# The 64x64 inverses of a chunked delta rule: substitution on 16x16 diagonal blocks instead of a Newton iteration

## The chip, the cores and the metric

The kernel runs on one core of a Trainium2 chip. The metric is the device time of one execution in microseconds (us); the fast executions of one kernel mostly agree within about 1%. Each experiment was timed in rounds beside the kernel before, on the same chip. The kernel before had a median of 325.67 us (323.14 to 328.43, three runs) when the change was predicted, and between 324.0 and 326.3 us in every later comparison.

## The reference

Causal linear attention with the delta rule (4 batches, 8 heads, 768 steps, head size 48), followed by an MLP over 3072 tokens (384 to 2048 to 384, GELU with tanh):

```python
k_n = k / (np.linalg.norm(k, axis=-1, keepdims=True) + 1e-06)
for t in range(S):
    y[:, :, t] = einsum('bhd,bhde->bhe', q[:, :, t], state)
    v_old = einsum('bhde,bhd->bhe', state, k_n[:, :, t])
    state = state + beta[:, :, t] * outer(k_n[:, :, t], v[:, :, t] - v_old)   # cut: index notation
x = y.transpose(0, 2, 1, 3).reshape(B * S, H * D)
out = gelu_tanh(x @ w_in) @ w_out
```

## The kernel before

The kernel works on chunks of 64 steps, 12 of them, with all 32 heads of a chunk at once: 16 head pairs, the two heads of a pair on partitions 0 to 63 and 64 to 127. Within a chunk the recursion is a triangular system: with the Gram matrix G of the 64 keys, the kernel needs the inverse T of (I + strict lower part of beta times G), one 64x64 matrix per head. T times R (values minus what the old state predicts) gives U, from which the new state S and the output x follow. One MLP tile takes the x of two chunks.

Before, T comes from a Newton iteration, five rounds of two products for each half of the heads:

```python
for j in range(5):                                   # cut: names of buffers, priorities
    op(..., {"pe": prod(h1, Zo, X)})                 # 16 products of 64x64
    op(..., {"dve": f_tt(F, 2I, v1(h1), ALU.subtract)})
    op(..., {"pe": prod(h2, F, Zo)})                 # 16 products of 64x64
    op(..., {"act": f_act(Z_next or TT, v1(h2))})
```

No instruction order is written by hand. Every operation is declared with an estimated cost for each engine that may run it, what it reads and writes, and a priority; a list scheduler in Python simulates the engines with these costs and fixes the order in which each engine's instructions stand:

```python
op(cost, fns, reads=..., writes=..., prio=..., alloc=[(bank, n)], dma=...)
...
P.schedule()      # one static order per engine, from the estimated costs
P.emit()          # semaphores between the engines
```

So each engine's list is fixed before the run. What that does shows in the timeline of the changed kernel further below: a product that TensorE had finished at about 251.1 us was read by VectorE only at 254.19, behind a transpose of 4.52 us.

Of the kernel before, what the change touches and what calls it, by code (L numbers as in the profile page):

```python
# [15 lines left out]
KEEP = 0.0  # L16
# [3 lines left out]

class Op:
    __slots__ = ("idx", "cost", "fns", "deps", "prio", "alloc", "uses", "dma", "lat",
                 "eng", "start", "end", "count", "clock", "sync", "mode", "bw")


class Plan:
# [14 lines left out]
    def op(self, cost, fns, reads=(), writes=(), prio=0.0, alloc=(), dma=None, lat=0.0, mode="t", bw=0.0):  # L41
        o = Op()
        o.idx = len(self.ops)
        o.cost, o.fns, o.prio, o.dma, o.lat, o.mode, o.bw = cost, fns, prio, dma, lat, mode, bw
        o.alloc = tuple(alloc)
        o.sync = set()
# [8 lines left out]
        for b in writes:  # L55
            if b in self.last_w:
                deps.add(self.last_w[b])
            deps.update(self.readers.get(b, ()))
# [14 lines left out]
    def schedule(self):  # L73
# [16 lines left out]
        pe_mode = "t"  # L90
# [28 lines left out]
        while n_left:  # L119
            pick = None  # L120
            for e in ENGINES:
# [3 lines left out]
                for i in ready[e]:  # L125
# [4 lines left out]
                    bb = []  # L130
                    if o.alloc:
                        ok = True
                        taken = []
                        for h, n in o.alloc:
                            sv = [(k, bank_free[k]) for k in taken]
                            for k in taken:
                                bank_free[k] = None
                            f = find_banks(n, t, *BANKS[o.mode])
                            for k, x in sv:
                                bank_free[k] = x  # L140
                            if f is None:
                                ok = False
                                break
                            bb.append((h, f[1], n))
                            taken += list(range(f[1], f[1] + n))
                            t = max(t, f[2] + 0.15)
                        if not ok:
                            continue
                    late = max(0.0, t - free_at[e])
                    pr = o.prio  # L150
                    if e == "pe" and (o.mode == "t") != (pe_mode == "t"):
                        pr += KEEP
                    far = late > NEAR[e]
                    key = (far, t if far else 0.0, pr, i)
                    if best is None or key < best[0]:
                        best = (key, i, t, bb)
# [6 lines left out]
            _, i, t, bb, e = pick  # L163
            o = ops[i]
            if e == "pe" and (o.mode == "t") != (pe_mode == "t"):
                t += SWITCH
                pe_mode = o.mode
            o.eng, o.start, o.end = e, t, t + o.cost[e]
# [31 lines left out]
    def emit(self):  # L200
# [21 lines left out]
        for _ in range(len(ops)):  # L222
# [12 lines left out]
            for d in o.deps | o.sync:  # L235
                p = ops[d]
                if p.eng == "pe" and e == "pe" and not p.dma:
# [74 lines left out]
def d_ps(n):  # L312
    return {"dve": 0.13 + 1.07e-3 * n}


def d_any(n):
    return {"act": 0.18 + 0.83e-3 * n, "dve": 0.13 + 1.07e-3 * n}
# [6 lines left out]
def d_pool2(n):  # L324
    return {"pool": 0.10 + 2.0e-3 * n}


def bass_deltanet__then__act_gelu_tanh_kernel(
# [12 lines left out]
    NP = NH // 2  # L341
    NCH = S // C
# [10 lines left out]
    with nc.allow_non_contiguous_dma("head rows"), nc.allow_low_precision("bf16 matmuls"):  # L353
# [3 lines left out]

        identF = sb("identF", [128, 128], F32)
        mU128 = sb("mU128", [128, 128], F32)
        idI = sb("idI", [128, 64], F32)  # L360
        mU = sb("mU", [128, 64], F32)
        half = sb("half", [128, NP], F32)
        BL = sb("BL", [128, 3, 2, 64], F32)
        bcol = sb("bcol", [128, NP, NCH], F32)
        RL, RB, NSQ = 3, 3, 3
        identB = sb("identB", [128, 64], BF16)
        twoI = sb("twoI", [128, 64], BF16)
# [3 lines left out]
        sq = [sb(f"sq{i}", [128, NP, D], F32) for i in range(2)]  # L371
# [3 lines left out]
        KQ = [sb(f"KQ{i}", [128, 2, NP, 64], BF16) for i in range(RB)]  # L375
        KQT = [sb(f"KQT{i}", [128, 2, NP // 2, 128], BF16) for i in range(RB)]
        NU = [sb(f"NU{i}", [128, NP, C], F32) for i in range(2)]

        def ring(nm, n, w):
            return [[[sb(f"{nm}{i}{g}{j}", [128, 8, w], BF16) for j in range(n)] for g in range(2)] for i in range(RB)]  # L380

        Nb, Wb, Xb, Zb, Fb = ring("N", 1, C), ring("W", 1, C), ring("X", 1, C), ring("Z", 2, C), ring("F", 1, C)
        DTb = [sb(f"DT{i}", [128, NP, C], BF16) for i in range(RB)]
        TT = [sb(f"TT{i}", [128, NP, C], BF16) for i in range(RB)]
        Rb = [sb(f"R{i}", [128, NP, D], BF16) for i in range(2)]
        Ub = [sb(f"U{i}", [128, NP, D], BF16) for i in range(2)]
        Sb = [sb(f"S{i}", [128, NP, D], BF16) for i in range(2)]
        x = sb("x", [128, 2, B, DM], BF16)
        xT = sb("xT", [128, 2, B * KT, 128], BF16)
# [19 lines left out]

        def aff(dst, cmp_, fill, pat, cm):  # L410
            return lambda g: g.affine_select(out=dst, in_=dst, compare_op=cmp_, fill=fill, base=0,
# [5 lines left out]

        op({"dve": 0.1}, {"dve": lambda e: e.memset(half[:, :], 0.5)}, writes=["half"], prio=-100)
        for i in range(RB):
            op({"dve": 0.7}, {"dve": lambda e, i=i: e.memset(KQ[i][:, :, :, D:64], 0.0)},  # L420
               writes=[f"KQz{i}"], prio=-90 + i)
        const("identF", identF, 0.0, ALU.not_equal, 1.0, [[-1, 128]], 1)
        const("mU128", mU128, 1.0, ALU.is_gt, 0.0, [[1, 128]], -1)
        for nm, big, sm in (("idI", identF, idI), ("mU", mU128, mU)):
            bn = {"mU": "mU128", "idI": "identF"}[nm]
            for a in range(2):
                r = slice(64 * a, 64 * a + 64)
                op({"dve": 0.1}, {"dve": f_cp(sm[r, :], big[r, r])}, reads=[bn], writes=[nm + str(a)], prio=-80)
        MASKU, IDI = ["mU0", "mU1"], ["idI0", "idI1"]
        op({"dve": 0.1}, {"dve": f_cp(identB[:, :], idI[:, :])}, reads=IDI, writes=["identB"], prio=-80)  # L430
        op({"dve": 0.1}, {"dve": lambda e: e.tensor_scalar(twoI[:, :], idI[:, :], 2.0, None, op0=ALU.mult)},
           reads=IDI, writes=["twoI"], prio=-80)

        bulk = []
# [14 lines left out]
        w1v = moe_w_in.rearrange("(kt p) f -> p kt f", p=128)  # L449
        w2v = moe_w_out.rearrange("(fc p) e -> p fc e", p=128)  # L450

        def load_w(nm, j, pr):
            if nm == "W1":
                dst, src, bw = W1[:, j, :], w1v[:, j, :], 2.9
            else:
                dst, src, bw = W2[:, 4 * j:4 * j + 4, :], w2v[:, 4 * j:4 * j + 4, :], 2.2
            op({"pool": 0.8}, {"pool": f_dma(dst, src)}, reads=gate(), writes=[f"{nm}{j}"], prio=pr,
               dma=f"d_{nm}{j}", bw=bw)
            bulk.append([f"{nm}{j}"])
# [13 lines left out]
        W1N = [f"W1{kt}" for kt in range(KT)]  # L473
        W2N = [f"W2{j}" for j in range(4)]

# [7 lines left out]
        op({"pe": 1.0}, {"pe": f_mms(bt_mms)}, mode="f", reads=["BL0", "BL1", "identF"], writes=[hb_ + (0,), hb_ + (1,)], alloc=[(hb_, 1)], prio=-50)  # L483
        for a in range(2):
            r = slice(64 * a, 64 * a + 64)
            op({"dve": 0.35}, {"dve": f_cp(bcol[r, :, :], lambda a=a, r=r: bank(hb_)[r, 0:NH * NCH].rearrange(
                "q (p a c) -> q p a c", a=2, c=NCH)[:, :, a, :])}, reads=[hb_ + (a,)], writes=[f"bcol{a}"], prio=-49)
        BCOL = ["bcol0", "bcol1"]


        def prep(c):
            s, i, j = c % RL, c % RB, c % 2
            pr = T(c, -STEP)
            kn = [f"kf{s}_0", f"kf{s}_1"]
            parts = [slice(0, 8), slice(8, 16)] if c == 0 else [slice(0, NP)]
            for n, u in enumerate(parts):
# [3 lines left out]
                op(cost, {"pool": f_tt(sq[j][:, u, :], kf[s][:, u, :], kf[s][:, u, :], ALU.mult),  # L500
                          "act": f_act(sq[j][:, u, :], kf[s][:, u, :], ACT.Square)},
                   reads=kn, writes=[f"sq{j}{n}"], prio=pr)
                op({"dve": 0.95 * w}, {"dve": lambda e, u=u: e.tensor_reduce(ss[j][:, u], sq[j][:, u, :], AX.X, ALU.add)},  # L503
                   reads=[f"sq{j}{n}"], writes=[f"ss{j}{n}"], prio=pr)
            ssn = [f"ss{j}{n}" for n in range(len(parts))]
            if c < NSQ:
# [9 lines left out]
            for n, u in enumerate(parts):  # L516
                w = 1.0 / len(parts)
                f = f_tt(KQ[i][:, 0, u, 0:D], kf[s][:, u, :],
                         rn[j][:, u].unsqueeze(2).to_broadcast([128, NP // len(parts), D]), ALU.mult)
                op({"dve": 0.9 * w} if c == 0 and n == 0 else {"pool": 1.5 * w}, {"pool": f, "dve": f},  # L520
                   reads=kn + [f"rn{j}", f"KQz{i}"], writes=[f"KQ{i}" if n == 0 else f"KQx{i}"], prio=pr)
            op({"pool": 0.85, "act": 0.82}, {"pool": f_cp(KQ[i][:, 1, :, 0:D], qf[s][:, :, :]),
                                             "act": f_act(KQ[i][:, 1, :, 0:D], qf[s][:, :, :])},
               reads=[f"qf{s}_0", f"qf{s}_1", f"KQz{i}"], writes=[f"KQq{i}"], prio=pr + 0.1)
            op({"sp": 1.1}, {"sp": f_dma(KQT[i].rearrange("p k m t -> p (k m) t"),
                                         KQ[i].rearrange("p k n d -> p (k n d)"), True)},
               reads=[f"KQ{i}", f"KQq{i}"] + ([f"KQx{i}"] if c == 0 else []), writes=[f"KQT{i}"], prio=pr + 0.2 if c > 1 else -50 + c, dma=f"d_T{c}", bw=1.5)

        def masks(c):
            j = c % 2  # L530
            pr = T(c, -STEP)
            op(d_pool2(NP * C), {"pool": f_tt(NU[j][:, :, :], mU[:, :].unsqueeze(1).to_broadcast([128, NP, C]),
                                              bcol[:, :, c:c + 1].to_broadcast([128, NP, C]), ALU.mult)},
               reads=MASKU + BCOL, writes=[f"NU{j}"], prio=pr + 0.3)

        def mm_pe(n_ins, cols, tiles=2):
            t = max(31.0, cols / 2.4 + 3.0) / tiles
            return {"pe": 1e-3 * n_ins * max(8.3, t)}
# [276 lines left out]
```

## Time and profile before

| kernel before | |
|---|---|
| time, median | 325.67 us |
| profiled span | 322.0 us |
| TensorE busy, products | 272.2 us, 7158 |
| VectorE, ScalarE, GpSimd busy | 175.0, 175.3, 127.1 us |
| start of R,TT of chunks 0, 1, 2, 3, 11 | 38.5, 60.4, 81.1, 112.6, 284.5 us |

The group R,TT (the product of T and R) occurs once per chunk, so its start is a milestone. The text speaks of a head (up to chunk 3), a steady stage (chunks 3 to 11) and a tail (MLP alone). In lines of the profile PE is TensorE (PEld its weight loads), DVE VectorE, ACT ScalarE, POOL GpSimd and SP SyncE, which issues transfers; a q marks an engine's instruction queue, and L with a number is a line of the kernel. One more line of the page before: the chain of work that ended last, by engine, as shares of the span.

```profile
PE 51%; DMA 22%; issue 7%; DVE 7%; ACT 5%; SPq 4%; POOL 2%; POOLq 0%
```

Half of the chain is TensorE, and VectorE has 7% of it.

### The profile page before, as it was taken

Reading aid. Unit: us, or ns where it says so; the run is one execution under the profiler, and the core shown is the slowest. Engines: PE = TensorE matmul, PEld = TensorE weight load, DVE = VectorE, ACT = ScalarE, POOL = GpSimd, SP = SyncE. Lnnn points to the kernel's source line nnn. Section 1 sums busy time; section 2 is a strip of 40 time slices with the busy share of each in tenths; the row PEclk is TensorE's granted clock in tenths of the full one; section 3 lists DMA queues with packets and bytes.
Section 4 is the critical chain, followed back from the end, with each engine's and each line's share of the span. In section 5 each row is a group of like instructions: output and inputs, shape, how many; then the busy total and the mean of one; then the engine's idle time right before and its main releaser. Section 6 shows DMA issues by size and latency. Waiting matters only on the chain.

```text
span 322.0 us, 15234 instructions
## 1 busy us (share of the span) xinstructions
PE 272.2 (85%) x7158; PEld 178.4 (55%) x7158; DVE 175.0 (54%) x279; ACT 175.3 (54%) x309; POOL 127.1 (39%) x96
## 2 busy tenths in 40 slices
PE   1158745988859789999899979989999999989995
PEld 1147644656636466666556556555566556544662
DVE  3489723767557467766775566674556554320111
ACT  4325543668447578634778443777345774168330
POOL 2842330877987257455546371260202211000000
PEclk9998775779998799999999999999999999999999
DMA  7998889879998435495557541709001002101022
GB/s 134 168 182 169 131 119 180 155 151 172 170 176 139 93 69 102 85 181 111 111 100 107 113 103 51 118 4 118 26 29 53 2 9 48 66 36 24 24 75 49
DMA packets 116206, 31.84 MB, mean 99 GB/s; under 512 B 110640, under 2 KB 115760, under 8 KB 116144
## 3 DMA queue, kind: packets, MB, share of 16 engines
q1 hardware_dynamic: 113600, 27.73, 45.5%
q0 software_dynamic: 2544, 3.15, 6.8%
q8 instruction: 56, 0.92, 1.2%
q14 instruction: 6, 0.05, 0.0%
HBM read 20.64 MB, written 4.72 MB: 79 GB/s over the span
## 4 chain that ended last, share of the span: by engine, by line
PE 51%; DMA 22%; issue 7%; DVE 7%; ACT 5%; SPq 4%; POOL 2%; POOLq 0%
PE ps L301 50%; DMA kf<-in_k_dram 8%; DMA qf<-in_q_dram 6%; DMA vf<-in_v_dram 4%; SPq L309 4%; DMA xT<-x 2%; DVE F L285 2%; DMA KQT<-KQ 1%; ACT Z L294 1%; ACT sq L294 1%; ACT x L294 1%; PE ps L600 1%; POOL sr L285 1%; DVE ss L503 1%; DVE R L285 1%
## 5 line engine op out<-in xcount | busy, mean ns | idle before, releaser
L285 DVE TENSOR_TENSOR F<-twoI,ps 128x512 bf16<-128x512 bf16 x120 | 80.4, 684 | 58.4 <-PE ps L301 57.7
L301 PE MATMUL ps<-xT,W 128*128 128x512 bf16 (+1 forms) x336 | 80.6, 364 | 1.8 <-ACT gT L294 1.0
L294 ACT ACTIVATE Z<-ps 128x512 bf16<-128x512 f32 x96 | 56.2, 595 | 42.3 <-PE ps L301 41.5
L294 ACT ACTIVATE gT<-ps 128x512 bf16<-128x512 f32 (+1 forms) x112 | 58.2, 536 | 32.3 <-PE ps L301 31.2
L301 PE MATMUL ps<-W,gT 128*128 128x384 bf16 x384 | 70.0, 327 | 0.6 <-ACT gT L294 0.6
L301 PE MATMUL ps<-X,Z 64*64 64x64 bf16 x1920 | 53.9, 201 | 12.8 <-ACT Z L294 6.9
L301 PE MATMUL ps<-Z,F 64*64 64x64 bf16 x1920 | 54.7, 201 | 8.7 <-DVE F L285 4.0
L301 PEld LDWEIGHTS ps<-X,Z 64*64 64x64 bf16 x1920 | 42.8, 116 | 29.8 <-ACT Z L294 15.1
L301 PEld LDWEIGHTS ps<-Z,F 64*64 64x64 bf16 x1920 | 43.0, 115 | 28.7 <-DVE F L285 15.8
L285 POOL TENSOR_TENSOR W<-identB,N 128x512 bf16<-128x512 bf16 x20 | 23.0, 1151 | 81.8 <-DVE N L285 78.1
L301 PEld LDWEIGHTS ps<-W,gT 128*128 128x128 bf16 x384 | 34.5, 98 | 21.8 <-ACT gT L294 0.8
L301 PEld LDWEIGHTS ps<-xT,W 128*128 128x128 bf16 x336 | 26.7, 100 | 23.1 <-ACT gT L294 4.2
L290 DVE COPY osb<-ps 128x384 f32<-128x384 f32 x20 | 11.1, 557 | 41.3 <-PE ps L301 41.3
L285 POOL TENSOR_TENSOR sr<-ss,half 128x16 f32<-128x16 f32 x9 | 26.2, 2911 | 5.4 <-DVE ss L503 5.2
L285 POOL TENSOR_TENSOR KQ<-kf,rn 128x768 bf16<-128x768 f32 (+1 forms) x12 | 17.1, 1423 | 21.2 <-PE ps L301 16.9
L285 POOL TENSOR_TENSOR NU<-mU,bcol 128x1024 f32<-128x1024 f32 x12 | 23.6, 1971 | 4.4 <-DVE N L285 4.0
L294 ACT ACTIVATE x<-ps 64x768 bf16<-64x768 f32 x24 | 19.3, 804 | 8.2 <-PE ps L301 7.9
L285 POOL TENSOR_TENSOR Z<-identB,N 128x512 bf16<-128x512 bf16 x20 | 23.0, 1151 | 0.0
L294 ACT ACTIVATE TT<-ps 128x512 bf16<-128x512 f32 x24 | 14.3, 596 | 13.4 <-PE ps L301 13.4
L294 ACT ACTIVATE X<-ps 128x512 bf16<-128x512 bf16 x24 | 14.3, 595 | 12.9 <-PE ps L600 12.9
L285 DVE TENSOR_TENSOR N<-ps,NU 128x512 bf16<-128x512 f32 x24 | 16.3, 686 | 8.6 <-PE ps L301 8.6
L301 PE MATMUL ps<-KQT 48*64 48x128 bf16 x384 | 12.7, 246 | 6.6 <-DMA KQT<-KQ 6.4
(49 smaller groups left out, 202.4 us busy)
## 6 DMA issues: line engine op xcount, KB each, us to landing
kf<-in_k_dram SPq DMA_DIRECT2D x24, 192.0 KB, 4.0
qf<-in_q_dram SPq DMA_DIRECT2D x24, 192.0 KB, 3.9
vf<-in_v_dram SPq DMA_DIRECT2D x24, 192.0 KB, 4.3
out_dram<-osb SPq DMA_DIRECT2D x20, 192.0 KB, 1.9
W<-in_moe_w_in_dram POOLq DMA_DIRECT2D x3, 512.0 KB, 6.0
W<-in_moe_w_out_dram POOLq DMA_DIRECT2D x4, 384.0 KB, 7.1
out_dram<-osb SPq DMA_DIRECT2D x8, 96.0 KB, 2.7
BL<-in_beta_dram SPq DMA_DIRECT2D x2, 96.0 KB, 3.6
```

The costliest lines, as they stand in the source:

```text
L285: return lambda e: e.tensor_tensor(out() if callable(out) else out, a() if callable(a) else a, b() if callable(b) else b, op)
L290: return lambda e: e.tensor_copy(out, a() if callable(a) else a)
L294: return lambda e: e.activation(out, a() if callable(a) else a, func)
L301: ins = t.matmul(out, lhsT, rhs, start=st, stop=sp_, skip_group_check=skip)
L309: return lambda e: e.dma_start(out, a)
L503: op({"dve": 0.95 * w}, {"dve": lambda e, u=u: e.tensor_reduce(ss[j][:, u], sq[j][:, u, :], AX.X, ALU.add)}, reads=[f"sq{j}{n}"], writes=[ ...
L600: ins = t.transpose(bankb()[r, p, :], W[r, p, :], identB[r, :])
```

## The change

The intent is to take work off TensorE. T is built from 16x16 diagonal blocks, which are inverted by substitution on GpSimd (VectorE for chunk 0), for two chunks at a time, a "pair". The kernel lays each block in one partition for that. So the 32x32 Gram blocks go through 32x32-block transposes on VectorE (Tt), then come 14 dependent steps of one multiplication and one addition, then two copies (XW, on ScalarE and GpSimd) and two transposes back (Dc). Two expansions (DI, WB) and four short block products on TensorE make T of it.

```diff
+            op({"dve": 1.25}, {"dve": lambda e: e.transpose(
+                Tt[j].rearrange("q (y x) i j -> q x j y i", y=2),
+                Gd[j].rearrange("q c p (x j) -> q x j c p", x=2))}, reads=nG, writes=[f"Tt{j}"], prio=pr)
+            sb_op(512, f_tt(X[:, :, :, :], Tt[j][:, 0:4:3, :, :], bM[j][:, :, :, :], ALU.mult), ...)
+            for s in range(14, 0, -1):
+                w = 15 - s
+                sb_op(2 * s * w, f_tt(tv, X[..., s:s+1], X[:, :, s:s+1, s+1:16], ALU.mult), ...)   # cut
+                sb_op(2 * s * w, f_tt(X[:, :, 0:s, s+1:16], X[:, :, 0:s, s+1:16], tv, ALU.add), ...)
+            ...
+            op({"act": 0.65}, {"act": f_act(XW[j][0].rearrange("q c b r -> q b r c"), X[:, :, :, :])}, ...)
+            for w in (1, 0):
+                op({"dve": 0.7}, {"dve": lambda e, w=w: e.transpose(
+                    Dc[j][w].rearrange("q c p j -> q j (c p)"), XW[j][w].rearrange("q j b i -> q j (b i)"))}, ...)
-            for j in range(5):
-                op(mm_pe(16, 64), {"pe": prod(h1, Zo, X)}, ...)        # cut: the Newton iteration
```

The rest, cut here: the scheduler gets a model of TensorE's instruction fetch (it counts 3.7 us for a block of 256 instructions; the 3.7 is the model's own number, and 2 x 7158 TensorE instructions over the 56 packets on the page before are 256 a packet), x is written transposed and completed by six small transfers per tile instead of one transposing transfer, the first three chunks transpose K and Q on TensorE, U,DT goes on four tiles of the array, W1 comes in eight loads instead of three, and the scheduler prefers to keep TensorE on a run of MLP products for at least 1.2 us and has a few other cost constants. All of this is in the kernel after; no run takes one of these parts away except the fetch model.

## The prediction

> **What bounds the kernel now.** I read the page's engine shares first, then its slices, the costliest groups, the waits of TensorE, and last the timeline of TensorE in the steady part.
>
> The engine shares and three rows of the slices (40 slices of 8.05 us each, busy tenths; the clock row is the granted TensorE clock):
>
> ```profile
> PE 272.2 (85%) x7158; PEld 178.4 (55%) x7158; DVE 175.0 (54%) x279; ACT 175.3 (54%) x309; POOL 127.1 (39%) x96
> ...
> PE   1158745988859789999899979989999999989995
> ...
> PEclk9998775779998799999999999999999999999999
> DMA  7998889879998435495557541709001002101022
> ```
>
> There are two stages. Up to slice 13 (about 105 us) the transfers are at 7 to 9 tenths and TensorE has holes, at a reduced clock. From slice 14 on TensorE is at 9 tenths, the clock is full and every other engine is below 8. So the head waits for data and chains of short operations, and the other 200 us are TensorE's instruction stream. The costliest groups say what that stream is (busy us, mean ns of one; the means contain pipeline overlap):
>
> ```profile
> L301 PE MATMUL ps<-X,Z 64*64 64x64 bf16 x1920 | 53.9, 201 | 12.8 <-ACT Z L294 6.9
> L301 PE MATMUL ps<-Z,F 64*64 64x64 bf16 x1920 | 54.7, 201 | 8.7 <-DVE F L285 4.0
> ```
>
> The two products of the Newton iteration for the 64x64 inverses are 3840 of 7158 matmuls and 109 of 272 busy us. Because ends of matmuls are modelled, I take costs from start to start in the timeline of TensorE (start us, duration us):
>
> ```profile
> 211.48 0.44 PE L301 MATMUL ps<-Z,F 64*64 64x64 bf16 x16
> 211.75 0.42 PE L301 MATMUL ps<-X,Z 64*64 64x64 bf16 x16
> 212.01 0.42 PE L600 MATMUL ps<-identB,W 64*64 64x64 bf16 x16
> ...
> 235.24 0.69 PE L301 MATMUL ps<-R,TT 64*64 64x48 bf16 x32
> 235.77 0.42 PE L301 MATMUL ps<-X,Z 64*64 64x64 bf16 x16
> 236.12 1.48 PE L301 MATMUL ps<-W,gT 128*128 128x384 bf16 x8
> 237.52 0.44 PE L301 MATMUL ps<-U,KQ 64*64 64x48 bf16 x32
> 237.80 0.66 PE L301 MATMUL ps<-U,DT 64*64 64x48 bf16 x32
> 238.30 0.42 PE L301 MATMUL ps<-Z,F 64*64 64x64 bf16 x16
> ```
>
> So 16 small products cost 0.27 us; 32 of them on two tiles of the array (R,TT) 0.53, on four tiles (U,KQ) 0.28. A run of 8 MLP products of N=384 occupies 1.40. Runs of N=512 occupy 0.75 for 3 and 1.40 for 6, so one is 0.216 and each run pays 0.10 once more than its products: the change between large and small products. The change back costs the same: X,Z at 235.77 is followed after 0.35, not 0.27. That leaves 0.163 for one of N=384; N=256 scales to 0.109.
>
> Check: a chunk is 64 time steps of all 32 heads, and an MLP tile takes the outputs of two chunks. A chunk before is 20 x 0.27 (Newton) + 2 x 0.27 (transposes) + 2 x 0.27 (Gram) + 0.53 + 0.51 + 3 x 0.28 = 8.3; its MLP share is (48 x 0.216 + 64 x 0.163) / 2 = 10.4; 224 changes over 12 chunks give 1.9. Sum 20.6. Measured: the R,TT groups start at 112.6 (chunk 3) and 284.5 (chunk 11), 21.5 per chunk. The steady stage is explained by TensorE's own instructions to 5%.
>
> [...] The queue of instructions (packets, MB, share of the 16 engines), and one row of the waits of TensorE (us in total, times, longest):
>
> ```profile
> q8 instruction: 56, 0.92, 1.2%
> PE ps L301 <- issue: 12.7, 12, 4.0
> ```
>
> [...] The second line is a wait of TensorE: 12.7 us in 12 stops, the longest 4.0, that no engine explains; I take them for blocks not yet there.
> [...] The trace has 827 ns against 558 for the 128x384 product KQ<-kf,rn, 1.5x. [...] a 128x16 tensor-scalar takes 230 ns here. [...]
>
> **The change part by part.**
> *Removed:* the Newton iteration: per chunk 5.4 us of TensorE, 0.54 of transposes, 10 VectorE operations F (684 ns), 8 Z and 2 X and 2 TT copies on ScalarE (0.6 each), the W and Z operations and the mask on GpSimd (4 x 1.15 + 1.97). Also the DMA transposes of x and, for three chunks, of K and Q.
> *Added on TensorE per chunk:* 64 32x32 products for the diagonal blocks (no such form in this trace; at the four-tile rate of 8.75 ns, an estimate of 0.55 us), four block products of 32 (0.53 each, 2.1). U,DT goes to four tiles (0.51 to 0.28). Sum small: 0.55 + 0.54 + 2.1 + 0.53 + 4 x 0.28 = 4.85 instead of 8.3. Changes of mode drop from 224 to 121, 1.0 per chunk. With the MLP unchanged at 10.4: **16.2 us per chunk** instead of 20.6.
> *Instruction fetch:* the order of instructions gives 5283 matmuls, 41 blocks instead of 56: less pressure, and the new scheduler spreads them.
> *Added on GpSimd per pair of chunks:* the rows sq (768: 1463 ns, 384: 825) give 0.19 us + 1.66 ns per element. Fourteen steps of multiply and add have 2240 elements: 28 x 0.19 + 3.7 = 9.0; each waits for the one before, say 0.06 each, 1.7; three 512-element operations (initial value, mask, scaling) 3.1; a memset 0.1. Sum 13.9. The rest of a pair: two K products and two pow (8.8), half of the squares and some casts (2.1). **24.8 of 32.5 us**, 76% busy: beside TensorE, not over it.
> *VectorE per chunk:* R, U, S (2.9), ET and three TT (3.0), two 1024-element expansions (1.6, from 0.41 for the 512-element bf16 W), DT (1.4), norms (1.4), transposes (1.3), output copies (1.0): 12.6 of 16.2, where it was 14.6 of 21.5. *ScalarE:* about 9.7.
>
> **The sum.** In the head the loads are the same, so I lay the chain out. Chunk 0 is solved on VectorE: K at 10 us, 3 for TensorE transposes and Gram, 1.3 transpose, 28 operations of about 0.3 with others between (12), 4 for transposes and expansions, 6 for the four products: R,TT near 39 us, as now (38.5). Chunks 1 and 2 are solved together on GpSimd, which first has to pass the gated weight loads (last issued at 45.9 now): 46 + 17 + 12 of products: R,TT near 75 and 80, where now it is 60.3 and 81.1. Chunks 3 and 4: about 108 and 113 (now chunk 3 at 112.6). So pairing gains nothing in the head. From 108 us there remain on TensorE about 9 x 4.85 = 44 of small products, tiles 2 to 6 (4 x 20.8 + 10.4 = 94), half of tile 1 (10), changes (10): 158, so 266; 4 for the last copies and stores; imperfect packing 3: a span of 273. The timed runs are 3.7 above the span (325.7 against 322.0): **276 us**.
>
> **Rivals.**
> 1. *GpSimd becomes the bound.* The chain per pair (transpose on VectorE, 28 dependent steps, transposes, expansions, products) is about 30 us long and nearly fills the 32.5 us of a pair; short strided rows are nowhere in this trace. If a step costs 0.5 instead of 0.33 us, the chain grows by 5 us per pair, over the 4.5 pairs from chunk 3 on: near 298. For it: the dependence and the in-order queue with 2.9 us pow operations between. Against: two pairs may be in flight (rings of 3 and 4).
> 2. *VectorE becomes the bound*, at 78% with short waits: products wait for ET and TT evictions. It adds about 1 us per chunk: 285.
> 3. *The head stays transfer-bound and TensorE colder.* [...] the head would end at 120 instead of 108: 287.
> 4. *More is gained:* x is ready without a DMA transpose (49.2 to 56.8 us now), so the MLP of tile 0 starts ten us earlier; if the head's holes fill up, 260.
>
> **Range and chances.** Rivals 1 to 3 push up by 10 to 25 and don't all add; rival 4 down by 15. Range 258 to 299. To miss 2% the chain would have to eat 43 of the 50 us: faster 0.93, same 0.05, slower 0.02.
>
> **What would show it.** Right: TensorE about 200 us busy, R,TT groups about 16 to 17.5 us apart after chunk 3, the last one near 232, a tail of 36 to 40 us of MLP alone; GpSimd below 80% in the steady part; 41 or 42 instruction packets. Wrong: small GpSimd operations well over 0.35 us start to start, TensorE waiting for TT or ET in the steady part (rival 1 or 2), chunk 3 later than 115 us (rival 3), or 32x32 groups of 64 taking over 0.8 us.

## The result, and the profile after

The changed kernel took **334.87 us** (median of four, 333.46 to 336.47) beside 326.34 us (323.14 to 328.43) of the kernel before in the same rounds. The ratio is 1.028, with a 95% interval of 1.020 to 1.036: slower, 59 us above the predicted 276 and 36 above the range. All ratios here are the mean time of one kernel's fast runs over that of the other's in the same rounds, so not quite the ratio of the medians quoted.

The page of the changed kernel: engine shares, then TensorE, VectorE and the granted clock (PEclk, the share of TensorE's full clock that the profile records, in tenths) in 40 slices of 8.3 us, then the chain that ended last.

```profile
PE 237.9 (72%) x5286; PEld 144.0 (43%) x5286; DVE 201.1 (61%) x268; ACT 134.2 (40%) x212; POOL 145.5 (44%) x252
...
PE   1611183584964495999667989579787959999995
...
DVE  5798748027669406987498844896499557510011
...
PEclk9999999998755567699998799699979987999999
...
PE 31%; DVE 27%; POOL 12%; ACT 10%; DMA 7%; issue 7%; SPq 6%
```

TensorE lost its work as intended, 272 to 238 us. But it now has holes in the steady stage, and in the chain VectorE stands at 27% instead of 7%. VectorE was to become lighter (14.6 to 12.6 us per chunk in the prediction); it went from 175 to 201 us busy. The costliest groups name why:

```profile
L738 DVE STREAM_TRANSPOSE Tt<-Gd 128x1024 bf16<-128x1024 bf16 x7 | 31.7, 4522 | 0.7 <-ACT Gd L339 0.7
L759 DVE STREAM_TRANSPOSE Dc<-XW 128x512 bf16<-128x512 bf16 x14 | 31.5, 2426 | 25.5 <-ACT XW L339 25.5
L339 ACT ACTIVATE XW<-Xf 128x512 bf16<-128x512 f32 x7 | 17.1, 2439 | 6.4 <-DVE Xf L751 5.0 <-POOL Xf L751 1.4
```

The columns after the bar are busy us and mean ns of one, then the idle time of the engine before them. The transposes take 63.2 us together, 5.3 per chunk; the prediction had 1.3 per chunk. The copy XW takes 2.44 us where other copies of 512 elements on ScalarE take 0.6. All three walk through memory with a stride: for each element of 2 bytes written, the next one lies 32 or 64 bytes away.

The timeline of the changed kernel around 240 us shows how they act in the chain of one pair (start us, duration us, engine; in brackets how long the engine had been idle, and for whom):

```profile
237.99 2.44 ACT L339 ACTIVATE XW<-Xf 128x512 bf16<-128x512 f32 x1 [0.67 <-POOL Xf L751]
...
240.47 4.51 DVE L759 STREAM_TRANSPOSE Dc<-XW 128x512 bf16<-128x512 bf16 x2 [2.28 <-ACT XW L339]
...
246.15 0.62 PE L346 MATMUL ps<-WB,G 64*64 64x48 bf16 x28 [1.26 <-DVE WB L330]
...
250.02 4.52 DVE L738 STREAM_TRANSPOSE Tt<-Gd 128x1024 bf16<-128x1024 bf16 x1
...
254.19 0.86 DVE L330 TENSOR_TENSOR TT<-ps,DI 128x512 bf16<-128x512 f32 x1
254.62 1.17 POOL L330 TENSOR_TENSOR Xf<-Tt,bM 128x512 f32<-128x512 bf16 x1 [15.31 <-DVE Tt L738]
255.11 0.67 PE L346 MATMUL ps<-TT,ET 64*64 64x16 bf16 x32 [2.32 <-DVE TT L330]
```

VectorE first waits 2.28 us for ScalarE's copy, then transposes for 4.51 us (two instructions), and soon for another 4.52 us for the next pair. The second transpose also holds up this pair: the eviction TT, VectorE's copy of a finished product out of the accumulators, stands behind it in VectorE's queue (its product, begun at 250.44 us, had ended at about 251.1), and TensorE waits 2.32 us for it with its next product. GpSimd has been idle for 15.31 us, of which the transpose itself takes the last 4.5. So the transposes delay work that does not depend on them.

Lines of the changed kernel that answer to others of the prediction. The queue of instructions on its page:

```profile
q8 instruction: 41, 0.67, 0.9%
```

the waits of TensorE that no engine explains:

```profile
PE ps L346 <- issue: 13.3, 10, 3.5
```

and two groups, the substitution's largest multiplication on GpSimd and the diagonal products on TensorE:

```profile
L330 POOL TENSOR_TENSOR tmp<-Xf 128x112 f32<-128x112 f32 x12 | 4.8, 399 | 0.8
...
L346 PE MATMUL ps<-KQT 48*32 48x32 bf16 x768 | 8.5, 188 | 6.3 <-issue 5.0 <-ACT KQT L339 1.3
```

The packets are the 41 that were predicted (2 x 5286 TensorE instructions over 41 are 258 a packet, 256 before), and the unexplained waits did not shrink with them (12.7 us before). That they are waits for instructions was the author's assumption: the trace names nothing that ended them. The two groups cost about what was estimated. The R,TT groups of chunks 0, 1, 2 start at 48.3, 94.2, 106.0 us, of chunk 3 at 144.7 and of chunk 11 at 287.6. That is 17.9 us per chunk in the steady stage (21.5 before, 16.2 to 17.5 predicted), but chunk 3 comes 32 us later than before, so most of the loss lies in the head.

### The profile page after: what moved, and what is told of

It is laid out like the page before. It is cut to its first block, busy times and chain, and to the rows that moved or that the text cites. A ratio compares the mean times of both kernels' runs of the same rounds, so it can differ in the third digit from the quotient of the medians.

```text
span 331.7 us, 11545 instructions
## 1 busy us (share of the span) xinstructions
PE 237.9 (72%) x5286; PEld 144.0 (43%) x5286; DVE 201.1 (61%) x268; ACT 134.2 (40%) x212; POOL 145.5 (44%) x252
## 4 chain that ended last, share of the span: by engine, by line
PE 31%; DVE 27%; POOL 12%; ACT 10%; DMA 7%; issue 7%; SPq 6%
PE ps L346 30%; DVE Dc L759 9%; SPq L354 6%; DVE Tt L738 5%; POOL Xf L330 5%; ACT XW L339 4%; POOL tmp L330 4%; DMA qf<-in_q_dram 3%; DMA kf<-in_k_dram 3%; DVE Xf L330 2%; DVE DT L697 2%; POOL sr L330 2%; DVE WB L330 2%; ACT x L339 2%; DVE DI L330 2%
## 5 line engine op out<-in xcount | busy, mean ns | idle before, releaser
L346 PE MATMUL ps<-x,W 128*128 128x512 bf16 (+1 forms) x336 | 85.5, 399 | 20.6 <-ACT gT L339 13.3
L346 PEld LDWEIGHTS ps<-x,W 128*128 128x128 bf16 x336 | 30.6, 107 | 61.6 <-ACT gT L339 27.8
L759 DVE STREAM_TRANSPOSE Dc<-XW 128x512 bf16<-128x512 bf16 x14 | 31.5, 2426 | 25.5 <-ACT XW L339 25.5
L346 PEld LDWEIGHTS ps<-W,gT 128*128 128x128 bf16 x384 | 36.2, 100 | 24.7 <-issue 2.2
L330 DVE TENSOR_TENSOR TT<-ps,DI 128x768 bf16<-128x768 f32 (+2 forms) x36 | 24.5, 700 | 12.8 <-PE ps L346 12.5
L738 DVE STREAM_TRANSPOSE Tt<-Gd 128x1024 bf16<-128x1024 bf16 x7 | 31.7, 4522 | 0.7 <-ACT Gd L339 0.7
L330 POOL TENSOR_TENSOR Xf<-Xf,tmp 128x28 f32<-128x28 f32 (+6 forms) x84 | 29.1, 346 | 5.7
L330 POOL TENSOR_TENSOR tmp<-Xf 128x28 f32<-128x28 f32 (+6 forms) x84 | 28.4, 338 | 6.0
L346 PE MATMUL ps<-KQT 48*32 48x32 bf16 (+1 forms) x1152 | 21.2, 215 | 11.4 <-issue 8.7
L330 POOL TENSOR_TENSOR Kn<-kf,rn 128x768 bf16<-128x768 f32 (+1 forms) x12 | 17.0, 1420 | 19.8 <-DVE rn L627 13.8
L330 POOL TENSOR_TENSOR Xf<-Tt,bM 128x512 f32<-128x512 bf16 x6 | 7.0, 1162 | 42.6 <-DVE Tt L738 42.6
L346 PE MATMUL ps<-WB,G 64*64 64x48 bf16 x384 | 10.5, 212 | 20.9 <-DVE WB L330 20.9
L346 PEld LDWEIGHTS ps<-KQT 48*32 48x32 bf16 (+1 forms) x1152 | 15.4, 107 | 16.3 <-issue 11.8
L346 PE MATMUL ps<-TT,ET 64*64 64x16 bf16 (+1 forms) x768 | 17.1, 181 | 7.2 <-DVE TT L330 4.9
L339 ACT ACTIVATE x<-ps 128x1024 bf16<-128x1024 f32 x12 | 12.6, 1051 | 21.7 <-PE ps L346 21.4
L346 PEld LDWEIGHTS ps<-TT,ET 64*64 64x64 bf16 x768 | 15.2, 116 | 12.3 <-DVE TT L330 7.2
```

The lines of the kernel that those rows point to most:

```text
L330: return lambda e: e.tensor_tensor(out() if callable(out) else out, a() if callable(a) else a, b() if callable(b) else b, op)
L339: return lambda e: e.activation(out, a() if callable(a) else a, func)
L346: ins = t.matmul(out, lhsT, rhs, start=st, stop=sp_, skip_group_check=skip)
L738: op({"dve": 1.25}, {"dve": lambda e: e.transpose(Tt[j].rearrange("q (y x) i j -> q x j y i", y=2), Gd[j].rearrange("q c p (x j) -> q x j ...
L759: op({"dve": 0.7}, {"dve": lambda e, w=w: e.transpose(Dc[j][w].rearrange("q c p j -> q j (c p)"), XW[j][w].rearrange("q j b i -> q j (b i) ...
```

## The experiments

Sixteen kernels ran. A first call held e1 to e4; there one run of the kernel before was unusually fast (319.4 us) and put most of the others into the slow state, so these four have no interval, and I compare medians (before 325.7).

**e1_flat: the same transposes and copy, without strides.** The result is wrong on purpose.

```diff
-                Tt[j].rearrange("q (y x) i j -> q x j y i", y=2),
-                Gd[j].rearrange("q c p (x j) -> q x j c p", x=2))}
+                Tt[j].rearrange("q (y x) i j -> q (y x i j)", y=2),
+                Gd[j].rearrange("q c p j -> q (c p j)"))}
-            ... f_act(XW[j][0].rearrange("q c b r -> q b r c"), X[:, :, :, :])
+            ... f_act(XW[j][0].rearrange("q c b r -> q (c b r)"), X.rearrange("q b i j -> q (b i j)"))
-            ... Dc[j][w].rearrange("q c p j -> q j (c p)"), XW[j][w].rearrange("q j b i -> q j (b i)")
+            ... Dc[j][w].rearrange("q c p j -> q (c p j)"), XW[j][w].rearrange("q j b i -> q (j b i)")
```

> Edit: the two kinds of 32x32-block transposes on VectorE (Tt and Dc) and ScalarE's copy XW read and write contiguously, same element counts, same order of instructions; the result is wrong on purpose. Theory (the strided 2-byte accesses of these three are the mis-sized term, on the serial chain of each pair): Tt 4.5 -> about 1.1 us, Dc 2.4 -> about 0.6, XW 2.4 -> about 0.6, so 8.5 us less per pair in the chain; R,TT of chunk 0 near 40 (48.3 now), of chunk 3 near 120 (144.7), time 285 to 300. Rival A (GpSimd's substitution is the bound): chain hardly moves after the head, time above 320. Rival B (the scheduler's order, made from wrong costs, is the trouble): the order is unchanged, so most of the loss stays, above 315.

Measured: 291.1 us (289.3 to 292.4). The groups of e1_flat in question:

```profile
L759 DVE STREAM_TRANSPOSE Dc<-XW 128x512 bf16<-128x512 bf16 x14 | 9.3, 696 | 13.7 <-ACT XW L339 13.4
L738 DVE STREAM_TRANSPOSE Tt<-Gd 128x1024 bf16<-128x1024 bf16 x7 | 8.6, 1235 | 0.7 <-ACT Gd L339 0.7
...
L339 ACT ACTIVATE XW<-Xf 128x512 bf16<-128x512 f32 x7 | 4.4, 628 | 6.1 <-DVE Xf L751 5.0 <-POOL Xf L751 1.0
```

The same instructions in the same order are 3.5 to 3.9 times shorter, and 43.7 of the 58.9 us between 334.9 and 276 are gone. The steady stage falls from 17.9 to 15.2 us per chunk, chunk 3 starts at 123.0. The theory holds, with its numbers.

**e2_costs: only the scheduler's estimates of the three operations are set to what they take.**

```diff
-            op({"dve": 1.25}, {"dve": lambda e: e.transpose(    # Tt
+            op({"dve": 4.55}, {"dve": lambda e: e.transpose(
-            op({"act": 0.65}, {"act": f_act(XW[j][0]...
+            op({"act": 2.45}, {"act": f_act(XW[j][0]...
-                op({"dve": 0.7}, {"dve": lambda e, w=w: e.transpose(    # Dc
+                op({"dve": 2.45}, {"dve": lambda e, w=w: e.transpose(
```

> Edit: only the scheduler's costs of Tt, Dc and XW are set to the measured 4.55, 2.45 and 2.45 us (1.25, 0.7 and 0.65 in the change); correct result. Theory (the operations themselves cost the time): the order improves a little, time 325 to 335, still no faster than before by 2%. Rival B (the loss comes from an order that was made for wrong costs): most of it comes back, time below 305.

Measured: 320.7 us (317.7 to 323.7), below what the theory expected: an order made for the true costs gives back 14 us, but leaves 45 of the 59. A wrong order is not the main cause. How much of the 14 is chance, see k2 and k3.

**e3_onestep: one substitution step of 14.**

```diff
-            for s in range(14, 0, -1):
+            for s in range(14, 13, -1):
```

> Edit: one of the 14 substitution steps instead of all, everything else kept; wrong result on purpose. Takes 26 small operations, about 10 us a pair, off GpSimd (off VectorE for chunk 0) and off the same serial chain that the transposes lie on; VectorE's load is unchanged for the pairs on GpSimd. Theory with the chain's latency as the limit: about the same gain as e1 (10 against 8.5 us per pair), 285 to 300. Rival A (GpSimd's occupancy is the bound): more than e1, below 280. Rival C (VectorE's occupancy is the bound, 201 us busy): little in the steady stage, above 315.

Measured: 324.4 us (321.7 to 325.1). This was counted as correct: the comparison with the reference is too loose to see the missing steps, so "correct" is weak evidence for a variant of this part. GpSimd's busy time fell from 145.5 to 91.8 us, about 9 per pair, and the time only by 10.5 us, as rival C expects. But the two stages differ. In the head chunk 3 starts at 123.8 us, 21 us earlier than in the changed kernel and within a microsecond of e1_flat. From chunk 3 to 11 the kernel needed 18.5 us per chunk, no less than with all steps; GpSimd's wait for Tt grew instead, from 42.6 us in the changed kernel to the 58.7 of this group of e3_onestep:

```profile
L330 POOL TENSOR_TENSOR Xf<-Tt,bM 128x512 f32<-128x512 bf16 x6 | 7.0, 1159 | 63.1 <-DVE Tt L738 58.7 <-DVE ss L625 4.4
```

So neither GpSimd's occupancy (rival 1 of the prediction) nor the latency of the pair's chain as such sets the steady pace, since this edit shortened the chain as much as e1_flat did. The head, on the other hand, answers to the length of this chain, whether it is the transposes or the steps that are shortened. What e1_flat gave back in the steady stage and e3_onestep did not is VectorE's time. The edit also let the scheduler choose another order, which e1_flat did not.

**e4_spare: four more strided transposes per pair, for nobody.**

```diff
+            for n in range(4):
+                op({"dve": 0.7}, {"dve": lambda e: e.transpose(
+                    spare.rearrange("q (m j) -> q j m", j=16), ...Gd[j]..., j=16))},
+                   reads=nG, writes=["BL0", "BL1"], prio=pr + 2.0)
```

> Edit: four more strided transposes of the size and form of Dc per pair, written to a buffer that nothing reads; correct result. VectorE gets about 4 x 2.4 = 9.7 us more per pair, while no operation of the chain waits for their data, but they stand in VectorE's in-order queue. If VectorE has slack in the steady stage (54% to 60% busy in the profile): 335 to 345. Rival C (VectorE's occupancy bounds): close to 9.7 x 7 = 68 us more, 385 or above. In between, say 360, its queue delays the chain.

Measured: 372.8 us (371.3 to 374.5), 38 more than the changed kernel. Nothing waits for the data of these transposes, yet 66.3 us of them cost 38. The page of e4_spare, engine shares and the added group:

```profile
PE 244.7 (66%) x5286; PEld 147.3 (40%) x5286; DVE 257.5 (69%) x291; ACT 140.3 (38%) x221; POOL 138.3 (37%) x248
...
L743 DVE STREAM_TRANSPOSE BL<-Gd 128x512 bf16<-128x512 bf16 x28 | 66.3, 2369 | 0.3
```

The total lies between the two expectations. By stages it is clearer: in the head the added transposes delay chunk 3 by 5 us, and the rest of the loss lies in the steady stage. The rows of the window from chunk 3 to chunk 11 (window, its length, busy us of TensorE, weight loads, VectorE, ScalarE, GpSimd, then granted clock, share of the transfer engines, GB/s), of the changed kernel, e4_spare and e1_flat:

```profile
144.67:287.62 142.95, 118.18 (x3073) 69.83 (x3072) 101.73 (x113) 60.72 (x91) 72.46 (x133) 0.92 0.39 72
149.85:329.01 179.16, 140.25 (x3236) 80.67 (x3237) 141.93 (x130) 68.45 (x102) 67.18 (x135) 0.84 0.33 61
123.02:244.68 121.66, 111.85 (x3073) 67.68 (x3072) 80.02 (x113) 53.72 (x91) 71.86 (x133) 0.97 0.48 86
```

Sixteen of the 28 useless transposes lie in this window, 38.4 us, and the window grew by 36.2 (its order is a new one, too). In e1_flat VectorE has 21.7 us less in it, and the window shrank by 21.3. Here VectorE's time shows almost whole in the pace, although it is busy only 71% in the changed kernel; that urgent work stands behind the long instructions in the static order, as in the timeline above, is the likely reason. This is rival 2 of the prediction, with a size that the prediction did not give it.

**f2_sides: is it the read or the write?** The stride is moved to the other side: Tt reads contiguously and writes with the stride, Dc and XW read with a stride and write contiguously. Wrong on purpose.

```diff
-                Gd[j].rearrange("q c p (x j) -> q x j c p", x=2))}
+                Gd[j].rearrange("q c p j -> q (c p j)"))}
-            XW: "q c b r -> q b r c"  <-  X
+            XW: "q c b r -> q c (b r)"  <-  X.rearrange("q b r c -> q c (b r)")
-            Dc: "q c p j -> q j (c p)"  <-  "q j b i -> q j (b i)"
+            Dc: "q c p j -> q (c p j)"  <-  flat XW.rearrange("q (t m) -> q m t", m=16)
```

> Edit: the stride is moved to one side: Tt reads contiguously and writes with the stride of the change, Dc and XW read with a stride and write contiguously; wrong result on purpose. If the strided write is what costs: Tt stays at about 4.5 us, Dc and XW fall to 0.6 to 1.2. If the strided read is what costs: Tt falls to about 1.2, Dc stays near 2.4. The time follows: with Tt alone slow, 3.9 us less per pair on VectorE than the change and 1.8 less on ScalarE, 300 to 315.

Measured: 317.5 us, ratio to before 0.974 (0.969 to 0.980; its profile fell in the slow state, so I use it for durations only), 2.5 us above the expected range. The groups of f2_sides in question:

```profile
L738 DVE STREAM_TRANSPOSE Tt<-Gd 128x1024 bf16<-128x1024 bf16 x7 | 31.4, 4488 | 1.0 <-ACT Gd L339 1.0
L759 DVE STREAM_TRANSPOSE Dc<-XW 128x512 bf16<-128x512 bf16 x14 | 14.6, 1083 | 16.1 <-ACT XW L339 16.1
...
L339 ACT ACTIVATE XW<-Xf 128x512 bf16<-128x512 f32 x7 | 7.5, 1069 | 5.1 <-DVE Xf L751 5.0 <-POOL Xf L751 0.2
```

The strided write of 2-byte elements is what costs. From e1_flat, 512 contiguous elements take 696 ns and 1024 take 1235, so 1.05 ns each and 157 ns per instruction. On top of these 157, Tt with the write alone strided takes 4.23 ns per element (4.26 with both sides strided), Dc with the read alone strided 1.81, with the write alone strided 4.43. ScalarE's copy shows the same: 628 ns contiguous, 1069 with a strided read of float32, 2439 with a strided write of 2-byte elements.

**f1_words: the same function, with pairs of bf16 moved as 32-bit words.** Two neighbours in memory form a word; the transposes move words (Tt 512, Dc 256), Tt is written contiguously, and XW is laid out in pairs.

```diff
-                Tt[j].rearrange("q (y x) i j -> q x j y i", y=2),
-                Gd[j].rearrange("q c p (x j) -> q x j c p", x=2))}
+                Tt[j].rearrange("q g k -> q (g k)").bitcast(WORD)[:, 0:512],          # WORD = int32
+                Gd[j]...bitcast(WORD).rearrange("q (cp w) -> q w cp", w=16))}
-                    Dc[j][w].rearrange("q c p j -> q j (c p)"), XW[j][w].rearrange("q j b i -> q j (b i)"))},
+                    Dc[j][w]...bitcast(WORD).rearrange("q (cp m) -> q m cp", m=8),
+                    XW[j][w]...bitcast(WORD).rearrange("q (m t) -> q m t", m=8))},
```

(Cut: two operations of GpSimd are split in halves, and the copy XW reads in pairs.)

> Edit: the same function as the change, but the transposes move neighbouring pairs of bf16 values as 32-bit words: Tt has 512 words, read with a stride and written contiguously; Dc has 256 words, read contiguously and written with a stride of 32 bytes; XW is written contiguously in pairs. Scheduler costs and order untouched except that two GpSimd operations of 512 elements become four of 256. Theory (each element of a strided 2-byte access costs 4 to 5 ns, and VectorE's queue passes that on): Tt 4.5 -> 0.7 to 1.3 us, Dc 2.4 -> 0.4 to 1.3, XW 2.4 -> about 0.65; time within 8 us of e1_flat's 291, so 283 to 300. If 32-bit transposes are no faster than 2-byte ones: 320 or more.

Measured: correct, 296.5 us, ratio to before **0.913** (0.908 to 0.918). Engine shares, granted clock and the chain by engine on the page of f1_words:

```profile
PE 220.6 (75%) x5261; PEld 140.3 (48%) x5286; DVE 156.8 (53%) x269; ACT 124.5 (42%) x216; POOL 144.7 (49%) x261
...
PEclk9999999979655559999999999799999999999999
...
PE 40%; DMA 22%; SPq 15%; POOL 7%; DVE 7%; issue 5%; ACT 4%
```

and the groups of f1_words in question:

```profile
L766 DVE STREAM_TRANSPOSE Dc<-XW 128x256 int32<-128x256 int32 x14 | 8.3, 633 | 13.2 <-ACT XW L340 10.2 <-POOL XW L331 2.8
L739 DVE STREAM_TRANSPOSE Tt<-Gd 128x512 int32<-128x512 int32 x7 | 7.2, 1028 | 0.0
L340 ACT ACTIVATE XW<-Xf 128x512 bf16<-128x512 f32 x7 | 4.5, 638 | 4.4 <-DVE Xf L756 4.3
```

The transposes now take 15.5 us, exactly the 1.3 per chunk of the prediction, and VectorE has 156.8 us, where the prediction's 12.6 per chunk make 151. In the chain that ended last VectorE is back at 7%. A strided word costs (1028 - 157) / 512 = 1.70 ns read and (633 - 157) / 256 = 1.86 ns written, for two elements each.

**f1c_i32 and f1c_f32: are the words moved bit by bit?** Two variants of f1_words compute each transpose both ways and add 1e6 times the difference to the data.

> Exactness of f1_words, which the loose comparison with the reference would not show (one substitution step of 14 still counts as correct): each word transpose (viewed as int32) is compared with the 2-byte transpose of the change on the chip, and 1e6 times the difference is added to the data. Correct only if the two agree bit by bit; its time is of no interest.

> The same test with the words viewed as float32. If it is correct, both views move bits unchanged; if it is wrong and the int32 view correct, words that read as denormals are altered by the float32 view.

Both were correct (367.7 and 368.9 us, with all the extra work). Both views move bits unchanged on this data. Words with an empty upper half do occur in it (in XW the diagonal of a triangular block stands beside a zero), and the float32 view did not alter them.

**What is left: 15 to 20 us in the head.** f1_words reaches chunk 3 at 126.7 us (108 predicted), then goes at 15.3 us per chunk (16.2 to 17.5 predicted), and has a tail of 45 us (36 to 40 predicted). The last two misses cancel: from chunk 3 to the end of the span it takes 167.6 us, where the prediction has 273 - 108 = 165. So nearly all that is left of the gap arises before chunk 3. Four kernels tried transfers, SyncE's queue and the fetch model, each as an edit of f1_words.

h1_xfer raises the scheduler's costs of transfers (for example `bw=1.05` to `1.3` for K, Q and V); no operation changes.

> What is left of the gap to the predicted 276: f1_words reaches chunk 3 at 126.7 us where 108 was predicted, and its chain in the head runs through loads of later chunks whose square sums and powers stand in front of urgent work in the in-order queues of VectorE and GpSimd. Edit on f1_words: only the scheduler's transfer and issue costs are raised to what the traces show (transfers by a quarter, K and Q transposes 2.2, x moves and stores 0.7 us of SyncE); no operation changes. If the order, made for transfers that are too fast, is the cause: chunk 3 by 118, time 280 to 290. If the head waits for the bytes themselves: no change within 2% of 296.

Measured: 298.8 us, ratio 0.924 (0.921 to 0.928). Chunks 1 and 2 came at 73.5 and 82.8 us, near the predicted 75 and 80, but chunk 3 again at 127, and the time is within 2% of 296, as the second expectation has it. It does not follow that the head waits for the bytes themselves: an order that expects slower transfers brings the first chunks earlier and gives it back by chunk 3.

h2_xact lets ScalarE issue the six small transfers of x (the 0.6 us each is the scheduler's cost; from 55.51 us of the changed kernel six of them take SyncE 4.28 us):

```diff
-                    op({"sp": 0.5}, {"sp": f_dma(xs[...], ...)},
+                    op({"act": 0.6}, {"act": f_dma(xs[...], ...)},
```

> Edit on f1_words: the six small transfers that complete x of a tile are issued by ScalarE (which wrote x) instead of SyncE, where they wait for x in front of the loads of the next chunks. If SyncE's queue in the head is the cause: 284 to 291 and chunk 3 earlier by 5 us or more; if not, 293 to 302 (ScalarE pays 6 times about 0.6 us per tile).

Measured: 294.9 us, ratio **0.909** (0.906 to 0.913), chunk 3 at 121.5. Chunk 3 is 5 us earlier, as the first expectation has it, but the time lies in the range of the second, and the interval overlaps that of f1_words: at most a small gain.

h4_both joins the two.

> h1_xfer and h2_xact together. If they act on different waits, the gains add: 272 to 284. If each removes the same wait, no better than the better of the two.

Measured: 311.0 us, ratio 0.960 (0.958 to 0.963). Neither expectation: together they lost 14 us against f1_words.

h3_nofetch sets the block time of the fetch model from 3.7 to 0.

> Edit on f1_words: the scheduler's model of instruction fetch is switched off (time of a block 0 instead of 3.7 us). The prediction gave the model no number, only fewer blocks. If it is worth something here: TensorE's unexplained waits grow and the time goes to 300 to 306. If it is worth nothing at this density of instructions: 293 to 300.

Measured: 305.6 us, ratio 0.943 (0.939 to 0.948). The unexplained waits of TensorE grew from 9.8 us in f1_words to those of the following line of h3_nofetch:

```profile
PE ps L347 <- issue: 16.1, 12, 2.1
```

**How far does chance of order go, and is the clock at fault?** The last call held four kernels.

e5_nofetch switches the fetch model off in the changed kernel itself.

> Edit on the changed kernel itself: the fetch model's block time 3.7 -> 0. If the model is worth some 9 us as on f1_words: 341 to 347 and more unexplained waits of TensorE (13.3 us now). If it only reshuffled the order by chance: either sign, and the unexplained waits within 2 us of 13.3.

Measured: 345.5 us, ratio 1.064 (1.060 to 1.068), 10.6 above the changed kernel, and unexplained waits of 17.5 us instead of 13.3.

k2_true and k3_xact_true set two costs in the scheduler, Tt from 1.25 to 1.05 and Dc from 0.7 to 0.65, in f1_words and in h2_xact.

> Edit on f1_words: the scheduler's cost of Tt 1.25 -> 1.05 and of Dc 0.7 -> 0.65, as measured for words. No operation changes. If chance of order is small: 293 to 300. If a trifle in the costs moves the time by 8 us or more either way, h3_nofetch's loss alone shows nothing of the fetch model.

> The same costs on h2_xact (294.9). Chance of order small: 291 to 298.

Measured: 297.6 us, ratio 0.911 (0.905 to 0.917), so nothing moved; and 303.6 us, ratio 0.937 (0.932 to 0.942), 8.7 us worse than h2_xact for a trifle in two costs, and outside its expectation. So a new order alone can cost 9 us. The fetch model's worth of 9 to 11 us is supported, twice with the same sign and with growing unexplained waits, but not shown. The same caution holds for the 14 us of e2_costs, and for h1_xfer and h4_both.

k1_warm fills gaps of TensorE between chunks 0 and 6 with idle products:

```diff
+        def warm(c):
+            for n in range(20):                       # two products of N=512, result unused
+                op({"pe": 0.45}, {"pe": f_mms(wm)}, ..., prio=T(c, 3000))
```

> Edit on f1_words: 120 idle products of N=512 (26 us at full clock) fill gaps of TensorE between chunks 0 and 6; results unused. If the clock dip to 0.5 to 0.6 near 100 to 130 us comes from TensorE having been idle before, the dip shrinks and the time stays within 5 us of 296.5 or falls. If the dip answers to work done [...], it comes earlier or grows longer and the time rises by 10 us or more.

Measured: 314.5 us, ratio 0.967 (0.960 to 0.973). Its granted clock, 40 slices of 7.8 us:

```profile
PEclk9999999999575999999959999989998799999999
```

The dip begins at the same place as in f1_words and does not go away, and the extra 26 us of work and the new order cost 18. In the trace's own clock records it lasts 20.5 us in two parts here and 34.1 us in f1_words, but also only 23.9 us in h1_xfer, which has no extra work. So this run is inconclusive: neither expectation came true, and the shorter dip may be chance of order.

The row misleads in the first slices: it shows 9 there, but the trace of f1_words holds no clock record before 58.1 us, that of the changed kernel none before 70.4, and that of the kernel before none before 26.9. Equal runs of products show how fast TensorE was. The kernel before, on either side of its first record:

```profile
26.50 0.60 PE L301 MATMUL ps<-Z,F 64*64 64x64 bf16 x16
27.39 0.44 PE L301 MATMUL ps<-Z,F 64*64 64x64 bf16 x16 [0.29 <-DVE F L285]
```

and f1_words, before its first record and late:

```profile
34.08 1.05 PE L347 MATMUL ps<-WB,G 64*64 64x48 bf16 x32 [9.38 <-DVE WB L331]
...
239.95 0.69 PE L347 MATMUL ps<-WB,G 64*64 64x48 bf16 x32
```

So TensorE was slower from the start until about its first clock record. What the later dip may cost, from the row of the window from 75 to 130 us of three kernels (columns as above), first before:

```profile
75.00:130.00 55.00, 46.53 (x1406) 30.20 (x1406) 35.33 (x58) 35.58 (x65) 38.47 (x25) 0.94 0.71 127
```

the changed kernel:

```profile
75.00:130.00 55.00, 35.75 (x987) 22.29 (x984) 31.96 (x37) 20.11 (x30) 31.90 (x43) 0.64 0.71 109
```

and f1_words:

```profile
75.00:130.00 55.00, 39.53 (x1214) 27.60 (x1220) 34.34 (x51) 19.85 (x33) 34.48 (x51) 0.69 0.70 100
```

If TensorE's busy time there scales with the clock, f1_words loses 39.5 x 0.31 = 12 us in this window and the kernel before 46.5 x 0.06 = 3. This is an estimate, and an upper one, since TensorE also waits there. It leaves out the slow products before 75 us. It would fit most of the head's 15 to 20 us, but no run separates it from the late loads.

## Why the prediction was wrong

**The mechanism on TensorE was right.** Newton's 3840 products went, the count of products and packets was as read from the order, and from chunk 3 on e1_flat and f1_words need 166 to 168 us, where 165 were predicted, once the transposes are short. (That the steady stage is faster than predicted and the tail longer cancels in this sum.) The diagonal products (768 of them, 8.5 us busy over the whole run) are as small as estimated.

**GpSimd was right.** The 28 steps of a pair that nothing interrupted (from 255.9 us in the changed kernel) took 11.8 us, 0.42 from start to start, against 10.7 in the prediction's sum, which is 0.38 each; the 0.33 that rival 1 names is the same sum without the wait. That wait, 0.06, was a guess; the first operation, at 255.86 us, takes 0.24 and the next starts at 256.18, so 0.08 here. The 827 and 558 ns that the prediction compares are GpSimd and VectorE on KQ<-kf,rn of 128x384 in the kernel before. GpSimd's total of 145.5 us fits 24.8 per pair. Rival 1 fell with e3_onestep for the steady stage; in the head the steps count like anything else in the chain.

**The step that failed is one term of a sum:** in the prediction's words "transposes (1.3)" among VectorE's costs per chunk, and "1.3 transpose" and "4 for transposes and expansions" in the head. No row of the profile stood behind it. The prediction named the 32x32 products and GpSimd's short rows as forms that the trace lacks, but not this one. It measured 5.3 per chunk, and ScalarE's copy, counted in "about 9.7" without a row of its own, 2.44 us instead of 0.63. The 1.3 is the scheduler's costs in the change, 1.25 and twice 0.7 us per pair, and e1_flat measured just these (1.24 and 0.70) for contiguous access. So the term assumed that a transpose moves elements at the usual rate whatever the strides; e1_flat and f2_sides show that the strided write of 2-byte elements runs at a quarter of it (4.2 to 4.4 ns against 1.05). The loss came in two ways: in the head through the length of the chain (chunk 3 at 144.7 us, 123.0 in e1_flat), in the steady stage through VectorE's time (17.9 us per chunk, 15.2 in e1_flat). With contiguous access the kernel takes 291.1 us and with words 296.5, both inside the predicted range of 258 to 299.

**Rival 2 was named and sized too small.** It took VectorE at 78% with short waits as worth 9 us (285 instead of 276). In the change VectorE was busy 71% of the steady stage (101.7 of 143 us) and set the pace all the same: of e4_spare's useless transposes the 38.4 us that fell in this stage made it 36 longer.

**The head was also too optimistic, by 15 us even with short transposes** (chunk 3 at 123 in e1_flat, 108 predicted). That is rival 3 in direction and about in size (its head ends at 120): at 75 to 130 us the granted clock ("colder" in the prediction is a lower one) was 0.64 in the changed kernel, 0.69 in f1_words and 0.94 before; what lowers it, no run shows. The sum for chunk 0 has a slip besides: its parts make 36.3 and not the 39 that are written, and 42.2 were measured in e1_flat and f1_words. "More is gained" (rival 4) did not happen. How the loss divides between the clock, late loads and the order stays open: h1_xfer, h2_xact, h4_both and k1_warm did not settle it. One reading of the page was loose too, without effect: ScalarE's row has an 8 in three slices after the 14th.

## What to carry to other kernels

A term of an estimate that has no row in the profile, above all a rearranging copy or transpose, deserves its own range, or a small measurement of exactly its access pattern. Write bf16 contiguously, with the stride on the read side if there must be one, or move pairs as 32-bit words (here an element took 1.05 ns contiguous, 1.81 read with a stride and 4.2 to 4.4 written with one, a strided word of two 1.70 to 1.86): that turned a kernel 2.8% slower than its predecessor into one 8.7 to 9.1% faster. An engine that is 60 to 70% busy in a static order may have no room for long instructions, even for those that nobody waits for: in e4_spare 38.4 us of them went with a steady stage 36.2 us longer, in which VectorE had been 71% busy; and a single changed order proves nothing below 9 us in this kernel.
